# Attention and gated MLP on one core: the planner's due time for loads of q and k, from the fifth pair on

## The chip, the cores and the metric

The kernel runs on one core of one Trainium2 chip. The metric is the time of one execution on the device in microseconds (us). The core's engines are PE (TensorE; the loading of its weights is shown apart as PEld), ACT (ScalarE), DVE (VectorE), POOL (GpSimd) and SP (SyncE, which here only issues transfers). Each engine works through its own list of instructions in order; an instruction that waits for another engine or for a transfer holds all those behind it.

## The reference

For 8 batches with 8 heads, 576 positions and head size 64, the heads' outputs go side by side into a gated MLP:

```python
q_rot, k_rot = rotate(q), rotate(k)                  # x1*cos - x2*sin, x1*sin + x2*cos
scores = q_rot @ k_rot.transpose(0, 1, 3, 2) / np.sqrt(D)
attn = np.exp(scores - np.max(scores, axis=-1, keepdims=True))
attn = attn / (np.sum(attn, axis=-1, keepdims=True) + 1e-09)
x = (attn @ v).transpose(0, 2, 1, 3).reshape(B, S, H * D)
h = np.maximum(x @ w_in, 0.0)
u, v = h[..., :d_ff // 2], h[..., d_ff // 2:]
v_n = (v - mean(v)) / np.sqrt(var(v) + 1e-06)
v_s = np.einsum('ts,bsd->btd', w_spatial, v_n) + b_spatial[None, :, None]
out = (u * v_s) @ w_out
```

## The kernel before

**The work.** Heads are taken two at a time: four pairs in each batch, 32 in all, `pairs[i]`, numbered 0 to 31. For each pair `prepare(i)` makes q and k ready, `attention(i)` does the scores, the softmax and the values, and after every fourth pair `mlp(b)` does the MLP of the batch, whose steps run beside the attention of the next batch. Most numbers are split into a rounded high part and the remaining low part, and products are made of the parts.

**The preparation of one pair** (from pair 3 on). Two transfers bring q and k into two stage buffers, `st{i}_0` for q and `st{i}_1` for k, 128 x 1152 numbers of 4 bytes each: the input half and its rotated half (line 306 issues every transfer by SP; in the trace `st<-in_qk_dram`). There are two stage buffers, so a load waits until the pair before is done with its own. Then POOL multiplies both halves by the tables (`rope`, L401) and adds them (`rope_sum`, L405), ACT rounds the sum to its high part (`round_hi`, L309), and POOL or DVE takes the low part (`rest_lo`, L312). Ten transfers copy the parts into the stacked operands `qs`, `ks` and `qz`, and the low part of k goes into `lk`. Only then can the pair's scores begin.

**The attention of one pair.** It goes in three chunks. For each tile PE makes the scores `sc` (L536, L546), DVE the negative row maximum `nmx` (L557), ACT the exponential `e` (L559). For each chunk and each of five blocks PE transposes the exponentials into `tp` (L576), ACT writes the high part `eh` from it (L587), DVE the low part `el` (L312; for the last, short block both go into one buffer named eh), and PE multiplies them by the values into `pv` (L600).

**The MLP of one batch.** PE makes `pa`, from which the norm comes (`vv`, `vn`), then `pb` (L767), which ACT turns into `u` (L770), then `pc` (L785), gated by DVE and POOL into `g`, and last `pd` (L800), which ACT copies into the output buffer `ob` (L803) for the transfer to memory. Four such buffers `ob{b}_0` to `ob{b}_3` are filled in two halves each.

**Buffers on PE's side.** The transposes `tp` and the MLP's `pa`, `pb`, `pc` and `pd` share three buffers, `pm`. One is free again when the last reader is done: ACT and DVE for `tp`, ACT for `pb` and `pd`. There are two buffers `sc` and one `pv`.

**What sets the order.** A planner writes the order of all instructions before the kernel runs. Every step is an `Op` with a cost for each engine that may do it and a `key`, its due time. `Program.run` plays the kernel through: whenever an engine is free, it takes the step with the smallest key among those whose inputs are ready and whose buffers can be had. A step's results count as ready after its cost and the engine's latency:

```python
LATENCY = {PE: 200, ACT: 142, DVE: 118, POOL: 95, DMA: 1700}
heapq.heappush(events, (now + chosen.costs[e] + LATENCY[e], n + 1, "done", chosen))
```

The times of this play only set the order; on the chip each instruction waits for its real inputs. The load of q or k has the cost 1640 and the key 20 * i - 27; for the norm, rope, sums and low parts the planner may also choose between POOL and DVE.

Of the kernel before, what the change touches and what calls it, by code (L numbers as in the profile page):

```python
# [17 lines left out]
S = 576  # L18
# [11 lines left out]
PE, ACT, DVE, POOL, DMA = "pe", "act", "dve", "pool", "dma"  # L30
LATENCY = {PE: 200, ACT: 142, DVE: 118, POOL: 95, DMA: 1700}
TO_PE = 105
SLOTS = {
    "stage": 2, "lk": 1, "vraw": 2, "vs": 2, "e2": 4, "e1": 2, "eh": 7, "rb": 1, "x32": 1, "xg": 7, "m": 4,
    "small": 3, "nmx": 3, "rt": 2, "sc": 2, "pv": 1, "pm": 3,
# [31 lines left out]
K_LOAD, K_ROPE, K_SUM, K_HIQ, K_LOQ, K_LOK, K_STACK, K_STACK2, K_V, K_VLO = 27, 8, 8, 9, 9, 11, 30, 8, -2, -9  # L67
# [20 lines left out]
class Buf:  # L88


    def __init__(self, pools, shape, dt, name):
        self.pools, self.shape, self.dt, self.name = pools.split(), shape, dt, name
        self.users, self.pool, self.slot, self.tile = 0, None, None, None
# [5 lines left out]
class Op:  # L99
    def __init__(self, costs, key, f, new, port):  # L100
        self.costs, self.key, self.f, self.new, self.port = costs, key, f, new, port
        self.eng = None
        self.waits, self.after, self.bufs = 0, [], []


class Program:
# [5 lines left out]
    def op(self, eng, ns, key, f, r=(), w=(), new=(), port=False):  # L112
        return self.either({eng: ns}, key, lambda e: f(), r, w, new, port)
# [23 lines left out]
    def run(self, make):  # L137
        free = {p: list(range(n)) for p, n in SLOTS.items()}
        ready = {e: [] for e in LATENCY}

        own = dict.fromkeys(SLOTS, 0)
        for o in self.ops:
            for b in o.new:
                own[b.pools[0]] += 1

        def place(bufs):

            taken = []
            for b in bufs:
                pool = next((p for n, p in enumerate(b.pools) if free[p] and not (n and own[p])), None)  # L150
                if pool is None:
                    for t in taken:
                        free[t.pool].insert(0, t.slot)
                    return False
                b.pool, b.slot = pool, free[pool].pop(0)
                taken.append(b)
            for b in bufs:
                own[b.pools[0]] -= 1
            return True

        busy = dict.fromkeys(LATENCY, False)
        held = dict.fromkeys(LATENCY, False)
        events = [(0, n, "ready", o) for n, o in enumerate(self.ops) if not o.waits]
        n, left = len(self.ops), len(self.ops)
        heapq.heapify(events)
        index = {o: k for k, o in enumerate(self.ops)}
        while events:
            now = events[0][0]
            while events and events[0][0] == now:
                _, _, what, o = heapq.heappop(events)  # L170
                if what == "ready":
                    for n_e, e in enumerate(o.costs):
                        heapq.heappush(ready[e], (o.key + STEAL * n_e, index[o], o))
                elif what == "free":
                    busy[o] = held[o] = False
                elif what == "place":
                    free[o.pool].append(o.slot)
                else:
                    for b in o.bufs:
                        b.users -= 1  # L180
                        if not b.users:
                            late = TO_PE if b.pool in PSUM and o.eng != PE else 0
                            heapq.heappush(events, (now + late, n, "place", b))
                            n += 1
                    for a in o.after:
                        a.waits -= 1
                        if not a.waits:
                            late = TO_PE if PE in a.costs and o.eng != PE else 0
                            heapq.heappush(events, (now + late, n, "ready", a))
                            n += 1  # L190
            for e in LATENCY:
                if busy[e]:
                    continue
                passed, chosen = [], None
                while ready[e] and not chosen:
                    item = heapq.heappop(ready[e])
                    if item[2].eng:
                        continue
                    other = {DVE: POOL, POOL: DVE}.get(e)
                    if item[2].port and other and held[other]:  # L200
                        passed.append(item)
                    elif place(item[2].new):
                        chosen = item[2]
                    else:
                        passed.append(item)
                for item in passed:
                    heapq.heappush(ready[e], item)
                if chosen:
                    for b in chosen.new:
                        b.tile = make(b)  # L210
                    chosen.eng = e
                    chosen.f(e)
                    left -= 1
                    busy[e], held[e] = True, chosen.port
                    heapq.heappush(events, (now + chosen.costs[e], n, "free", e))
                    heapq.heappush(events, (now + chosen.costs[e] + LATENCY[e], n + 1, "done", chosen))
                    n += 2
        assert not left, "instructions wait for each other"
        return now
# [3 lines left out]
def tile_attention_gated_mlp(  # L223
# [33 lines left out]
    op = prog.op  # L257
# [47 lines left out]
    def load(dst, src):  # L305
        nc.sync.dma_start(out=dst, in_=src)  # L306
# [74 lines left out]
    def prepare(i):  # L381
        b, hp = pairs[i]
        key = 20 * i
        if i < WHOLE:
            return prepare_whole(i, b, hp, key)
        st = [Buf("stage", [P, 2 * S + TW], F32, f"st{i}_{j}") for j in range(2)]
# [19 lines left out]
            pair_op(S, key - K_SUM, f, first=eng, r=[(st[j], 1)], w=[(st[j], 0)])  # L406

        for j in range(2):
            op(DMA, 1640, key - K_LOAD, lambda j=j: load(st[j][:, :2 * S], qk[b, hp, j].rearrange("p c n -> p (c n)")), w=[(st[j], 0), (st[j], 1)], new=[st[j]])
        op(DMA, 910, key - K_LOAD + 1, lambda: load(vr.tile, v[b, hp]), w=[vr], new=[vr])  # L410
        for j, eng, part in ROPE0 if b == 0 else ROPE:
            if part is None:
# [435 lines left out]
    prepped, xs, chain = [], [], []  # L848
    op(POOL, 800, -26, setup, w=["ident", "bias", ("sums", 0, 0), ("sums", 1, 0), ("qz", 0), ("qz", 1), ("qs", 0, 0), ("qs", 1, 0)])
    prepare(0)  # L850
    for c in range(4):
        decode(DEC_V[c], win, (1, c), w_in[c * P:(c + 1) * P, 2 * HF:4 * HF])
# [7 lines left out]
    for i in range(len(pairs)):  # L860
        if i:
            prepare(i)
        (attention_plain if i < PLAIN else attention)(i)
        if i % NP == NP - 1:
            mlp(i // NP)
# [68 lines left out]
```

## Time and profile before

| | |
|---|---|
| median of 3 runs | 981.48 us (977.74 to 984.55) |
| profiled execution | 979.22 us |
| its span | 977.4 us |
| mean granted clock of TensorE | 0.999 of full speed |
| PE busy | 942.1 us, 96% |
| PEld busy | 853.3 us, 87% |
| ACT busy | 733.9 us, 75% |
| DVE busy | 672.1 us, 69% |
| POOL busy | 571.6 us, 58% |

The profile is of one execution, and its span leaves out what lies around it, here some 2 us. A busy share over the whole span mixes the start, when weights are decoded and PE waits, with the batches behind it, which look much alike, some 116 us each; a stretch of one batch says more. The lists of waits say for which instruction of which other engine an engine stood idle, how long in total, how often, and the longest.

### The profile page before, as it was taken

The page shows a single profiled execution, that of the slowest core. Times are in us where ns is not written, and L with a number is a line of the kernel's source. Part 1 is how long each engine was busy: PE and PEld are TensorE (multiplying, and loading weights), DVE is VectorE, ACT ScalarE, POOL GpSimd, SP SyncE. Part 2 cuts the span into 40 slices and gives each one's busy share as a digit, 9 for nine tenths or more (in the row PEclk, how much of TensorE's full clock was granted, in tenths as well). Part 3 has the DMA queues.
Part 4 walks back from the last instruction along what each step waited for, and adds up shares of the span by engine and source line. Part 5 has one row for each costly group of instructions (what it writes and reads, how often), then busy time and mean ns, then how long its engine had stood idle before and what let it go on. Part 6 is the DMA issues. An engine that isn't in the chain of part 4 may idle for free.

```text
span 977.4 us, 19421 instructions
## 1 busy us (share of the span) xinstructions
PE 942.1 (96%) x6618; PEld 853.3 (87%) x6618; DVE 672.1 (69%) x1486; ACT 733.9 (75%) x1827; POOL 571.6 (58%) x500
## 2 busy tenths in 40 slices
PE   4999999999999999999999999999999999999998
PEld 2455689998899989999899988999889998999998
DVE  6999898765866677675776658676686756767331
ACT  3778788777987779776897768877798677976452
POOL 5852445556757657774756766666576765672121
PEclk9999999999999999999999999999999999999999
DMA  7761733454344553345444444445524455330101
GB/s 295 221 197 52 209 100 108 130 128 140 99 139 117 153 150 101 111 120 165 120 130 108 118 151 126 118 128 149 139 76 132 126 156 145 98 93 17 62 2 49
DMA packets 54581, 121.56 MB, mean 124 GB/s; under 512 B 12881, under 2 KB 12881, under 8 KB 54482
## 3 DMA queue, kind: packets, MB, share of 16 engines
q1 hardware_dynamic: 54482, 120.32, 43.1%
q8 instruction: 53, 0.87, 0.4%
q14 instruction: 46, 0.38, 0.1%
HBM read 66.03 MB, written 9.58 MB: 77 GB/s over the span
## 4 chain that ended last, share of the span: by engine, by line
PE 59%; ACT 14%; DMA 9%; DVE 8%; POOL 4%; issue 3%; SPq 2%; DVEq 0%; ACTq 0%; POOLq 0%
PE pc L785 12%; PE sc L536 9%; PE pv L600 8%; PE tp L576 8%; PE pd L800 7%; PE pa L744 4%; PE pb L767 4%; ACT e L559 4%; DMA qs<-st 3%; POOL st L401 2%; ACT eh L587 2%; DVE nmx L557 2%; SPq L306 2%; PE sc L546 2%; ACT vv L827 2%
## 5 line engine op out<-in xcount | busy, mean ns | idle before, releaser
L587 ACT ACTIVATE eh<-tp 128x384 fp32r<-128x384 f32 (+1 forms) x504 | 217.5, 433 | 85.6 <-PE tp L576 69.5
L312 DVE TENSOR_TENSOR el<-tp,eh 128x384 fp32r<-128x384 f32 x336 | 185.9, 554 | 105.1 <-ACT eh L587 92.6
L559 ACT ACTIVATE e<-sc,nmx 128x576 f32<-128x576 f32 x288 | 213.0, 741 | 39.1 <-DVE nmx L557 36.7
L557 DVE TENSOR_REDUCE nmx<-sc 128x1 f32<-128x576 f32 x288 | 215.2, 749 | 31.8 <-PE sc L536 23.4
L576 PE MATMUL tp<-ident,e 128*128 128x128 f32 (+1 forms) x1176 | 197.1, 273 | 11.6 <-ACT ob L803 7.7
L576 PEld LDWEIGHTS tp<-ident,e 128*128 128x128 f32 (+1 forms) x1176 | 144.5, 138 | 30.4 <-ACT ob L803 9.1
L401 POOL TENSOR_TENSOR st<-st,tabq 128x576 f32<-128x576 f32 x55 | 77.7, 1427 | 135.9 <-DMA st<-in_qk_dram 131.0
L600 PE MATMUL pv<-eh,vs 128*128 128x384 f32 (+1 forms) x560 | 154.0, 316 | 0.1
L785 PE MATMUL pc<-wsp,vn 128*128 128x288 f32 x768 | 143.3, 304 | 0.8 <-DVE u L843 0.5
L767 PE MATMUL pb<-x,wi 128*128 128x288 f32 x768 | 142.3, 306 | 0.7 <-ACT u L770 0.7
L800 PE MATMUL pd<-g,wo 128*128 128x288 f32 x768 | 140.8, 304 | 0.0
L744 PE MATMUL pa<-wi,x 128*128 128x512 f32 x448 | 133.0, 407 | 0.0
L536 PE MATMUL sc<-ks,qs 128*128 128x288 f32 x580 | 123.2, 302 | 0.0
L785 PEld LDWEIGHTS pc<-wsp,vn 128*128 128x128 f32 x768 | 115.0, 189 | 3.4 <-DVE u L843 0.9
L710 POOL TENSOR_TENSOR x<-x,rb 128x576 f32<-128x576 f32 x31 | 44.3, 1429 | 123.7 <-DVE x L615 93.4
L767 PEld LDWEIGHTS pb<-x,wi 128*128 128x128 f32 x768 | 112.3, 189 | 4.4 <-PE pb L767 1.4
L800 PEld LDWEIGHTS pd<-g,wo 128*128 128x128 f32 x768 | 113.5, 189 | 2.6
L600 PE MATMUL pv<-el,vs 128*64 128x384 f32 (+1 forms) x448 | 113.7, 295 | 0.0
L536 PE MATMUL sc<-lk,qz 128*128 128x288 f32 x522 | 111.9, 295 | 0.0
L600 PEld LDWEIGHTS pv<-eh,vs 128*128 128x128 f32 x560 | 97.7, 188 | 5.8 <-DVE x L615 1.6
L312 DVE TENSOR_TENSOR eh<-tp,eh 64x256 fp32r<-64x256 f32 (+1 forms) x168 | 59.8, 356 | 61.4 <-ACT eh L587 52.3
L536 PEld LDWEIGHTS sc<-ks,qs 128*128 128x128 f32 x580 | 93.1, 189 | 6.3 <-ACT e L559 0.8
(180 smaller groups left out, 1559.2 us busy)
## 6 DMA issues: line engine op xcount, KB each, us to landing
st<-in_qk_dram SPq DMA_DIRECT2D x63, 576.0 KB
ks<-st SPq DMA_DIRECT2D x116, 160.0 KB
qs<-st SPq DMA_DIRECT2D x116, 144.0 KB
vr<-in_v_dram SPq DMA_DIRECT2D x32, 320.0 KB
out_dram<-ob SPq DMA_DIRECT2D x32, 288.0 KB
qz<-st SPq DMA_DIRECT2D x58, 144.0 KB
ws<-in_w_spT_dram SPq DMA_DIRECT2D x2, 576.0 KB
st<-in_qk_dram SPq DMA_DIRECT2D x2, 288.0 KB
```

The lines of the kernel that those rows point to most:

```text
L312: eng.tensor_tensor(out=lo, in0=src, in1=hi.bitcast(F32), op=ALU.subtract)
L401: f = lambda e: e.tensor_tensor(out=st[j][:, cols], in0=st[j][:, cols], in1=(tabs if j else tabq)[:, cols], op=ALU.mult)
L536: nc.tensor.matmul(pt[:, c * 512:c * 512 + HALF], lhsT=lhsT, rhs=rhs[:, k0 + c * HALF:k0 + (c + 1) * HALF], start=(n == 0), stop=(n == len ...
L557: op(DVE, 665, key + K_MAX, lambda: nc.vector.tensor_reduce(out=nmx.tile, in_=tops(), op=ALU.max, axis=AX.XY, negate=True), r=[pt], w=[nmx ...
L559: op(ACT, 730, key + K_EXP, lambda: nc.scalar.activation(e[:, e0:e0 + S].rearrange("p (c n) -> p c n", c=2), tops(), AF.Exp, bias=nmx.tile ...
L576: nc.tensor.transpose(out=tp[:e.shape[1], m * P:m * P + P], in_=e, identity=ident)
L587: nc.scalar.activation(h, p, AF.Copy)
L600: nc.tensor.matmul(pv[0:rows, c1:c2], lhsT=vs[:, kt, h, vp, :], rhs=part[:, c1:c2], start=(kt == 0 and n == 0 and c1 == 0), stop=last)
L744: nc.tensor.matmul(pm.tile, lhsT=lhsT, rhs=win[1, d][:, j, :], start=(d == 0 and n == 0), stop=(d == 3 and n == len(todo) - 1))
L767: nc.tensor.matmul(pm[:, :HALF], lhsT=win[0, d][:, i, f * P:(f + 1) * P], rhs=x[d][:, at:at + HALF], start=(d == 0 and n == 0), stop=(d == ...
L785: nc.tensor.matmul(pm[:, :HALF], lhsT=lhsT, rhs=rhs, start=(t == 0 and n == 0), stop=(t == 4 and n == 1))
L800: nc.tensor.matmul(pm[:, :HALF], lhsT=wout[d,][:, i, m * P:(m + 1) * P], rhs=gs[d][:, at:at + HALF], start=(d == 0 and n == 0), stop=(d == ...
```

## The change

The planner's `Op` gets a number `late`, zero by default, and a step's results count as ready so much later. The loads of q and k get 1500 ns from the fifth pair (i = 4) on: for the planner their data are there 1640 + 1700 + 1500 = 4840 ns after the issue instead of 3340. No instruction of the chip is added or taken away.

```diff
@@ -30,6 +30,7 @@
 PE, ACT, DVE, POOL, DMA = "pe", "act", "dve", "pool", "dma"
 LATENCY = {PE: 200, ACT: 142, DVE: 118, POOL: 95, DMA: 1700}
 TO_PE = 105
+LATE = 1500
 SLOTS = {
     "stage": 2, "lk": 1, "vraw": 2, "vs": 2, "e2": 4, "e1": 2, "eh": 7, "rb": 1, "x32": 1, "xg": 7, "m": 4,
     "small": 3, "nmx": 3, "rt": 2, "sc": 2, "pv": 1, "pm": 3,
@@ -99,7 +100,7 @@
 class Op:
     def __init__(self, costs, key, f, new, port):
         self.costs, self.key, self.f, self.new, self.port = costs, key, f, new, port
-        self.eng = None
+        self.eng, self.late = None, 0
         self.waits, self.after, self.bufs = 0, [], []
 
 
@@ -213,7 +214,7 @@
                     left -= 1
                     busy[e], held[e] = True, chosen.port
                     heapq.heappush(events, (now + chosen.costs[e], n, "free", e))
-                    heapq.heappush(events, (now + chosen.costs[e] + LATENCY[e], n + 1, "done", chosen))
+                    heapq.heappush(events, (now + chosen.costs[e] + LATENCY[e] + chosen.late, n + 1, "done", chosen))
                     n += 2
         assert not left, "instructions wait for each other"
         return now
@@ -406,7 +407,8 @@
             pair_op(S, key - K_SUM, f, first=eng, r=[(st[j], 1)], w=[(st[j], 0)])
 
         for j in range(2):
-            op(DMA, 1640, key - K_LOAD, lambda j=j: load(st[j][:, :2 * S], qk[b, hp, j].rearrange("p c n -> p (c n)")), w=[(st[j], 0), (st[j], 1)], new=[st[j]])
+            o = op(DMA, 1640, key - K_LOAD, lambda j=j: load(st[j][:, :2 * S], qk[b, hp, j].rearrange("p c n -> p (c n)")), w=[(st[j], 0), (st[j], 1)], new=[st[j]])
+            o.late = LATE if i >= 4 else 0
         op(DMA, 910, key - K_LOAD + 1, lambda: load(vr.tile, v[b, hp]), w=[vr], new=[vr])
         for j, eng, part in ROPE0 if b == 0 else ROPE:
             if part is None:
```

In the changed file the lines behind the new constant are one further down, and those from the loads on two.

The instructions are the same, but for three operations of pairs 3 to 7 and batch 0 that go from DVE to POOL. The lists have 3454 rows on PE, and about 200 of them stand elsewhere; 509 on SP, one of them elsewhere. The order differs from about 107 us of the trace before on. From the third batch on the differences repeat in every batch, one kind for each of its four pairs, and the end from about 870 us on is as it was.

In the rows below a name is followed by its batch, pair, head, chunk, block or half, and a serial number at the end. Before, on ACT, in batch 4's output (`pd4`, `ob4`) beside pairs 23 and 24, while pair 25 is prepared:

```order
L617 ACTIVATE avt23_1_9744<-pv23_1_9627 64x384
L803 ACTIVATE ob4_2_9752<-pd4_20_9702 128x288
L587 ACTIVATE eh23_2_3_9779<-tp23_2_3_9770 128x384
L559 ACTIVATE e2_24_1_9784,sums0_68<-sc24_0_3_9754,nmx24_0_3_9774 128x576
L309 ACTIVATE st25_0_9645<-st25_0_9645 128x576
L803 ACTIVATE ob4_2_9752<-pd4_21_9746 128x288
L587 ACTIVATE eh23_2_4_9808<-tp23_2_4_9800 64x2x128
L587 ACTIVATE eh23_2_4_9808<-tp23_2_4_9800 64x128
L587 ACTIVATE eh24_0_0_9817<-tp24_0_0_9811 128x384
L803 ACTIVATE ob4_3_9844<-pd4_30_9795 128x288
L309 ACTIVATE st25_1_9671<-st25_1_9671 128x576
```

The rounding of pair 25's q stands ahead of the copy of `pd4_21`. The same place on ACT in the changed kernel:

```order
L589 ACTIVATE eh23_2_3_9778<-tp23_2_3_9749 128x384
L561 ACTIVATE e2_24_1_9789,sums0_68<-sc24_0_3_9768,nmx24_0_3_9776 128x576
L805 ACTIVATE ob4_2_9737<-pd4_21_9743 128x288
L310 ACTIVATE st25_0_9638<-st25_0_9638 128x576
L589 ACTIVATE eh23_2_4_9811<-tp23_2_4_9799 64x2x128
L589 ACTIVATE eh23_2_4_9811<-tp23_2_4_9799 64x128
L589 ACTIVATE eh24_0_0_9820<-tp24_0_0_9807 128x384
L805 ACTIVATE ob4_3_9844<-pd4_30_9793 128x288
L589 ACTIVATE eh24_0_1_9851<-tp24_0_1_9840 128x384
L561 ACTIVATE e2_24_1_9789,sums0_68<-sc24_0_4_9824,nmx24_0_4_9838 128x576
L310 ACTIVATE st25_1_9660<-st25_1_9660 128x576
```

The copy now stands ahead of the rounding of q, and two more rows stand ahead of that of k. It is so at the pairs 9, 13, 17, 21, 25 and 29. Before, on ACT, two pairs earlier, while batch 4's `u` is made:

```order
L587 ACTIVATE eh21_2_3_8925<-tp21_2_3_8916 128x384
L559 ACTIVATE e2_22_1_8930,sums0_68<-sc22_0_3_8899,nmx22_0_3_8920 128x576
L309 ACTIVATE st23_0_8787<-st23_0_8787 128x576
L770 ACTIVATE u4_3_8945<-pb4_30_8891 128x288
L587 ACTIVATE eh21_2_4_8954<-tp21_2_4_8947 64x2x128
L587 ACTIVATE eh21_2_4_8954<-tp21_2_4_8947 64x128
L587 ACTIVATE eh22_0_0_8963<-tp22_0_0_8957 128x384
```

The rounding of pair 23's q stands ahead of `u4_3`. The same place on ACT in the changed kernel:

```order
L589 ACTIVATE eh21_2_3_8924<-tp21_2_3_8915 128x384
L561 ACTIVATE e2_22_1_8929,sums0_68<-sc22_0_3_8898,nmx22_0_3_8919 128x576
L772 ACTIVATE u4_3_8939<-pb4_30_8890 128x288
L589 ACTIVATE eh21_2_4_8952<-tp21_2_4_8945 64x2x128
L589 ACTIVATE eh21_2_4_8952<-tp21_2_4_8945 64x128
L310 ACTIVATE st23_0_8787<-st23_0_8787 128x576
L589 ACTIVATE eh22_0_0_8967<-tp22_0_0_8955 128x384
```

It now stands behind `u4_3` and the two pieces of `eh21_2_4`, and so at the pairs 11, 15, 19, 23, 27 and 31. Before, on POOL, in the preparation of pair 22:

```order
L401 TENSOR_TENSOR st22_0_8311<-st22_0_8311,tabq_65 128x576 x2
L312 TENSOR_TENSOR vn_73<-vv4_0_8264,vn_73 128x512
L405 TENSOR_TENSOR st22_0_8311<-st22_0_8311 128x576
L401 TENSOR_TENSOR st22_1_8337<-st22_1_8337,tabs_64 128x576 x2
L312 TENSOR_TENSOR vn_73<-vv4_1_8297,vn_73 128x512
L405 TENSOR_TENSOR st22_1_8337<-st22_1_8337 128x576
L312 TENSOR_TENSOR st22_0_8311<-st22_0_8311 128x576
```

The last two rows are the sum of k and the low part of q. The same place on POOL in the changed kernel:

```order
L402 TENSOR_TENSOR st22_0_8311<-st22_0_8311,tabq_65 128x576
L313 TENSOR_TENSOR vn_73<-vv4_0_8264,vn_73 128x512
L402 TENSOR_TENSOR st22_0_8311<-st22_0_8311,tabq_65 128x576
L402 TENSOR_TENSOR st22_1_8337<-st22_1_8337,tabs_64 128x576
L406 TENSOR_TENSOR st22_0_8311<-st22_0_8311 128x576
L313 TENSOR_TENSOR vn_73<-vv4_1_8297,vn_73 128x512
L402 TENSOR_TENSOR st22_1_8337<-st22_1_8337,tabs_64 128x576
L313 TENSOR_TENSOR st22_0_8311<-st22_0_8311 128x576
L406 TENSOR_TENSOR st22_1_8337<-st22_1_8337 128x576
```

The low parts of the norm (`vn`) stand between the ropes, and the sum of k stands behind the low part of q; so it is at the pairs 10, 14, 18, 22, 26 and 30.

## Rows read from the trace of the kernel before

**Rows 1.** The page's first part: busy us, share of the span, instructions of each engine.

```profile
PE 942.1 (96%) x6618; PEld 853.3 (87%) x6618; DVE 672.1 (69%) x1486; ACT 733.9 (75%) x1827; POOL 571.6 (58%) x500
```

**Rows 2.** Windows: busy us (instructions) of each engine, PE clock, DMA share, GB/s.

```profile
core 0: us, PE busy (x) PEld busy (x) DVE busy (x) ACT busy (x) POOL busy (x), PEclk, DMA share, GB/s
...
100.00:227.00 127.00, 123.65 (x881) 110.69 (x877) 99.05 (x208) 97.63 (x242) 68.31 (x57) 1.00 0.49 135
573.00:689.00 116.00, 113.70 (x826) 107.47 (x826) 79.43 (x182) 91.59 (x231) 75.69 (x65) 1.00 0.46 127
```

**Rows 3.** Waits of PE from 100 to 900 us: total us, times, longest.

```profile
PE tp L576 <- ACT ob L803: 7.7, 6, 1.5
PE tp L576 <- ACT u L770: 2.1, 3, 0.8
PE tp L576 <- DVE eh L312: 0.6, 1, 0.6
PE pc L785 <- DVE u L843: 0.5, 1, 0.5
PE pb L767 <- ACT u L770: 0.5, 1, 0.5
```

**Rows 4.** Waits of POOL and of ACT over the whole span.

```profile
POOL st L401 <- DMA st<-in_qk_dram: 131.0, 24, 7.9
ACT st L309 <- POOL st L405: 15.0, 24, 1.6
```

**Rows 5.** Timeline: start us, us, engine, line, operation [idle before <- releaser], 686.6 to 692 us.

```profile
686.75 0.65 PE L800 MATMUL pd<-g,wo 128*128 128x288 f32 x3
...
687.77 0.68 ACT L309 ACTIVATE st<-st 128x576 fp32r<-128x576 f32 x1 [1.60 <-POOL st L405]
688.36 0.39 ACT L803 ACTIVATE ob<-pd 128x288 f32<-128x288 f32 x1
688.65 1.23 ACT L587 ACTIVATE eh<-tp 64x256 fp32r<-64x256 f32 x3
...
688.80 0.55 PE L576 MATMUL tp<-ident,e 128*128 128x128 f32 x3 [1.40 <-ACT ob L803]
...
689.33 0.72 DVE L312 TENSOR_TENSOR eh<-tp,eh 64x256 fp32r<-64x256 f32 x2 [3.29 <-ACT eh L587]
...
691.13 0.49 PE L576 MATMUL tp<-ident,e 128*128 128x128 f32 x3
...
691.38 0.65 PE L800 MATMUL pd<-g,wo 128*128 128x288 f32 x3
...
691.87 0.33 PE L600 MATMUL pv<-eh,vs 128*128 128x384 f32 x1
```

**Rows 6.** Timeline, 630.2 to 631.7 us.

```profile
630.28 0.68 ACT L309 ACTIVATE st<-st 128x576 fp32r<-128x576 f32 x1 [0.91 <-POOL st L405]
630.87 0.39 ACT L770 ACTIVATE u<-pb 128x288 f32<-128x288 f32 x1
631.16 0.65 ACT L587 ACTIVATE eh<-tp 64x256 fp32r<-64x256 f32 x2
...
631.31 0.55 PE L576 MATMUL tp<-ident,e 128*128 128x128 f32 x3 [0.73 <-ACT u L770]
```

**Rows 7.** Timeline of SP: loads of pairs 22 and 25, first copies of pair 25's k.

```profile
589.88 1.78 SPq L306 DMA_DIRECT2D st<-in_qk_dram  x2
...
677.23 2.55 SPq L306 DMA_DIRECT2D st<-in_qk_dram  x2
...
692.75 1.10 SPq L306 DMA_DIRECT2D ks<-st  x2
```

**Rows 8.** Timeline of POOL: ropes of pairs 22 and 25, low part of pair 22's q.

```profile
593.64 2.83 POOL L401 TENSOR_TENSOR st<-st,tabq 128x576 f32<-128x576 f32 x2 [5.84 <-DMA st<-in_qk_dram]
...
604.46 1.44 POOL L312 TENSOR_TENSOR st<-st 128x576 fp32r<-128x576 f32 x1
...
682.16 2.82 POOL L401 TENSOR_TENSOR st<-st,tabq 128x576 f32<-128x576 f32 x2 [7.83 <-DMA st<-in_qk_dram]
```

**Rows 9.** Timeline of ACT: both pieces of pair 22's k rounded.

```profile
607.09 0.82 ACT L309 ACTIVATE st<-st 128x576 fp32r<-128x576 f32 x2
```

**Rows 10.** Timeline of PE: first score of pair 25.

```profile
705.45 0.43 PE L536 MATMUL sc<-ks,qs 128*128 128x288 f32 x2
```

## What the change will do: a prediction

> **What bounds the kernel now.** I read the busy shares first. PE works 942.1 of 977.4 us [rows 1], and in a settled stretch of one batch 113.70 of 116 us, while ACT has 91.59 and DVE 79.43 [rows 2]. So PE sets the time, and since the change keeps every instruction, it can pay only by taking idle time from PE; idle time of POOL, ACT or DVE counts only where PE is behind it.
>
> Next I read what PE waits for between 100 and 900 us [rows 3]. Two lines carry it: the transposes (L576) wait six times for ACT's output copy ob (L803), 7.7 us in all, and three times for ACT's u (L770), 2.1 us. The smaller lines below them all lie in batch 0, before 227 us. Asked apart, the stretch from 227 us on has the first two lines and no other. The rest of PE's 35 idle microseconds lies at the start and at the end, where the order of the instructions that run then is hardly touched.
>
> Why does PE wait for an output copy? The stall at 688.80 us shows it [rows 5]. PE begins its last three pd matmuls before it at 686.75 and then has no work until 688.80, when the transposes of pair 24, chunk 0 start, released by the ob copy that began at 688.36. The copy frees one of three pm buffers. The copy itself had its input long before. It stood behind the rounding of pair 25's q (L309, 687.77), which had waited 1.60 us for POOL's sum (L405). ACT takes its queue in order. POOL in turn was late because the load of that pair was late: POOL's ropes (L401) wait for q and k loads 24 times, 131.0 us in all, and ACT's roundings for POOL's sum 24 times, 15.0 us [rows 4]. At 631.31 us the same thing happens with u in the place of ob: 0.91 us of waiting on ACT, 0.73 on PE [rows 6].
>
> How late is the load? The one for pair 25 is issued at 677.23 [rows 7], and POOL's first rope on it starts at 682.16, ending a wait of 7.83 us for just that [rows 8]: 4.93 us. For pair 22 it is 589.88 to 593.64, 3.76 us. The plan counts 1640 + 1700 ns = 3.34 us. By it the rounding stood ready before the copy, so the copy was put behind it; on the chip it is not ready, by 1.6 us there.
>
> **The change part by part.** The plan now counts 4.84 us for those loads, close to the 4.93 at the place that stalls.
>
> *Six places with ob (pairs 9, 13, ... 29).* In the new order ACT's ob copy stands ahead of the rounding that waits. The pm buffer is then free as soon as pd is done, and the transposes no longer wait: six waits, 7.7 us [rows 3].
>
> *Three places with u (the pairs 4n+3).* The order puts u and the two pieces of eh ahead of the rounding: 2.1 us [rows 3].
>
> *What the restart costs besides.* From the start of the three pd matmuls at 691.38 to the next matmul's at 691.87 is 0.49 us; from 686.75 the next could have started at 687.24, and it started at 688.80. That is 1.56 us where the row's idle time says 1.40 [rows 5]: 0.16 us more per stall, by nine stalls 1.4 us. Together 7.7 + 2.1 + 1.4 = 11.2 us.
>
> *What is late next.* ACT still waits at the ob places, now with the copy done. Behind its rounding stand the two short pieces of eh, and behind them DVE's subtraction (689.33, 0.72 us), which frees the pm buffer for the transposes now at 691.13 [rows 5]. Without the copy in front, eh starts at 688.36 instead of 688.65, and DVE is done at 689.33 - 0.29 + 0.72 = 689.76. With PE earlier by 1.56, those transposes want the buffer at 691.13 - 1.56 = 689.57. So 0.2 us comes back, if POOL is as late as it is now. The bounds are nothing (POOL a little earlier) and 0.3 us (one more handover), by six places 0 to 1.8; I take 0.8. At the u places eh stands ahead of the rounding as well, so nothing comes back there.
>
> *The rounding that is now later.* Pair 25's q is rounded later by the copy, 0.39 us [rows 5], and at the u places by u and eh, 0.39 + 0.65 us [rows 6]. Who waits for that? The copies of q and k into the stacked operands, and then the pair's first score on PE. For pair 25 the first k copies are issued at 692.75 [rows 7] and the score starts at 705.45 [rows 10]: some 12 us of cover. I cost it at nothing; without the cover it would be at most 1.04 us at each of 12 places.
>
> *POOL and DVE, pairs 4n+2.* Sum of k moves behind the low part of q on POOL. Before, the low part ends at 604.46 + 1.44 = 605.90 [rows 8] and ACT comes to its roundings at 607.09 [rows 9] without waiting. If POOL does the same work in the new order and ends its last piece then, 1.2 us of slack remains. Nothing, as long as the load lands as it does.
>
> *SP.* Its order keeps all 509 entries, one of them moved; no queue of transfers is held by the change. Whether a q or k load is issued earlier depends on when its stage buffer is free, which is not new.
>
> *Batch 0 (105 to 185 us).* Here the reordering is wide, and three operations go from DVE to POOL. PE is idle for 127.00 - 123.65 = 3.35 us between 100 and 227 us [rows 2], so a gain is at most about 3. A loss of the same size is as near, from a new wait as long as the longest two there are [rows 3]. I take 0, with both ends kept.
>
> **Sum.** The profiled execution took 979.22 us, against the runs' median of 981.48, 2.26 lower and within their spread. 979.22 - 11.2 + 0.8 = 968.8 on its own footing; with the 2.26 put back, 971.0 us, a ratio of 0.989. Batch 0 (3 either way) and the part that comes back (0.8 down, 1.0 up) give 967 to 975.
>
> One rule of the Trainium skill speaks against the change. Its page "DMA: Bandwidth & Descriptors", section "Anatomy of one DMA — SWDGE (gpsimd) path", fits one transfer as 2.0 us plus its bytes over 436,000 per us. For 589,824 bytes I estimate 3.35 us from it, which is the old plan's figure to 10 ns; by it the old order would be right and the sum nothing. That section is about another issuing path, and the trace differs: 4.93 and 3.76 us [rows 7, 8].
>
> **The rivals.** *The wait moves on.* The rounding still blocks ACT at the six ob places, and if what is behind it (eh, DVE, the pm buffer) is 0.5 to 1.2 us late instead of 0.2, then 3 to 7 of the 11.2 us are lost again. For it: three pm buffers turn fast, and ACT's idle 1.60 us has not gone anywhere [rows 5]. Against it: the 0.2 us worked out above. Time: 975 to 980.
>
> *The plan counts too much.* Half of the loads land in about 3.8 us like pair 22's [rows 7, 8]; for them 4.84 is wrong by 1.1. If that delays work that PE needs at as many places as it frees, the sum is nothing: 978 to 984. Against it: PE has no wait on the loads' chain other than through ACT's queue [rows 3], and the cover of 12 us.
>
> *Slower: sum of k at the pairs 4n+2 (7 places from pair 6 on).* It now stands last on POOL, with 1.2 us of slack before ACT reaches the rounding of k. A load that lands in 4.96 us instead of 3.76 uses it up; pair 25's took 4.93. Beyond it, each microsecond holds ACT, whose queue there has the softmax's work for PE behind it. To eat the 10.4 us of net gain takes 1.5 us at each of seven places, so loads of 6.5 us; at 7.1 us it is 7 x 2.1 = 15 us, 984 on the profile's footing and 986 for the median. The rows hold no such load.
>
> **How the numbers follow.** The forecast, 967 to 975, has 0.62: mechanism and rows agree nine times. The wait that moves on has 0.23, the plan that counts too much 0.07, slower 0.08. About 1% is what a measurement of this kernel can tell from no change, so faster starts below 971.7: two thirds of the forecast's case, 0.41. Slower by over 1% is the last rival, 0.08 with little of the others; the rest, 0.51, lies within. The range 966 to 979.5 holds the forecast and nearly all of the wait that moves on, and leaves out the slower case and most of the plan that counts too much.
>
> **What would show it.** In the profile after, PE's line of transposes waiting for ob should be gone or under 1 us, that for u gone, and ACT's waits of L309 for L405 still there, some 10 us or more, with ob and u ahead of them. PE busy in a batch should be near 115 of 116 us. A new line, transposes waiting for DVE's eh, of up to 2 us would be the part that comes back; over 3 us it is the first rival. Waits of ACT on the rounding of k at the pairs 4n+2, with PE behind, would be the last one. I am wrong if PE's total wait is as before, or if the loads themselves land later now.

## The result, and the profile after

The changed kernel took 968.24 us in the median (967.76 to 968.79) against 983.01 of the kernel before beside it: a ratio of 0.9851, interval 0.9816 to 0.9885. Its profiled execution took 968.03 us, before 979.22. So it is faster by 1.1 to 1.8%; 971.0 was forecast, within 966.0 to 979.5. One execution of one experiment below (after, transfer added: 1008.68 us at a granted clock of 0.884) was in a slower state of the chip and is left out of the ratios.

The page's first part, answering to [rows 1]: PE does the same work in a span 11.1 us shorter.

```profile
PE 940.3 (97%) x6618; PEld 853.8 (88%) x6618; DVE 667.7 (69%) x1484; ACT 734.7 (76%) x1828; POOL 572.3 (59%) x501
```

Windows of the kernel after, columns as in [rows 2]: batch 0 has 1.51 us without PE instead of 3.35, a settled stretch 0.17.

```profile
100.00:226.00 126.00, 124.49 (x892) 112.17 (x893) 95.86 (x210) 99.66 (x251) 69.86 (x59) 1.00 0.51 139
455.00:569.00 114.00, 113.83 (x829) 107.97 (x828) 79.88 (x183) 92.09 (x232) 76.04 (x65) 1.00 0.48 130
```

Waits of PE after, from 100 to 890 us. The two lines that led [rows 3] are gone. One of the two waits of the first line, 0.65 us, is told of below; the other lies in batch 0.

```profile
PE tp L578 <- DVE eh L313: 0.8, 2, 0.7
PE tp_2a L637 <- DVE et_1b L646: 0.7, 1, 0.7
PE pc L787 <- DVE u L845: 0.3, 1, 0.3
...
```

Waits of POOL and ACT after, over the whole span, against [rows 4]. POOL waits for late loads as ever (some of its waits now bear the name of another transfer), but ACT's waits for POOL's sum are down to 10 from 24: it comes to the rounding later, with other work done first. Only one of the ten, 1.32 us at pair 25, is at a place with ob or u ahead of q's rounding. Five, of 1.23 to 1.25 us, are at the pairs 12, 16, 20, 24 and 28, where before had 0.2 to 0.6: POOL comes to their first rope 5.5 to 5.8 us after the issue of the load instead of 3.9 to 4.0. No wait of PE follows those five.

```profile
POOL st L402 <- DMA st<-in_qk_dram: 109.8, 18, 7.3
...
POOL st L402 <- DMA rt23d<-rt: 8.8, 1, 8.8
...
ACT st L310 <- POOL st L406: 8.6, 10, 1.3
```

The place with `u`, against [rows 6], first on ACT (timeline of the kernel after): u, both pieces of eh, then the rounding of pair 23's q, without a wait. PE's transposes of pair 22 start at 623.01, with no idle time ahead of them.

```profile
621.85 0.41 ACT L772 ACTIVATE u<-pb 128x288 f32<-128x288 f32 x1
622.80 0.66 ACT L589 ACTIVATE eh<-tp 64x256 fp32r<-64x256 f32 x2 [0.55 <-PE tp L578]
623.49 0.69 ACT L310 ACTIVATE st<-st 128x576 fp32r<-128x576 f32 x1
```

A place with `ob` as five of the six look now, pair 21's (timeline of ACT after): the copy, and right behind it the rounding, which by then has its input.

```profile
564.69 0.40 ACT L805 ACTIVATE ob<-pd 128x288 f32<-128x288 f32 x1
564.98 0.68 ACT L310 ACTIVATE st<-st 128x576 fp32r<-128x576 f32 x1
565.55 1.17 ACT L589 ACTIVATE eh<-tp 64x256 fp32r<-64x256 f32 x3
```

The sixth, pair 25's, against [rows 5] (timeline of all engines after). The copy is done early and PE starts pair 24's transposes at 678.94 with no wait. The rounding still waits 1.32 us, and behind it stand eh, DVE's subtraction, and PE's next transposes, 0.65 us late.

```profile
678.15 0.41 ACT L805 ACTIVATE ob<-pd 128x288 f32<-128x288 f32 x1
...
678.94 0.49 PE L578 MATMUL tp<-ident,e 128*128 128x128 f32 x3
...
679.88 0.69 ACT L310 ACTIVATE st<-st 128x576 fp32r<-128x576 f32 x1 [1.32 <-POOL st L406]
...
680.48 1.16 ACT L589 ACTIVATE eh<-tp 64x256 fp32r<-64x256 f32 x3
...
681.15 0.73 DVE L313 TENSOR_TENSOR eh<-tp,eh 64x256 fp32r<-64x256 f32 x2 [3.30 <-ACT eh L589]
...
682.03 0.52 PE L578 MATMUL tp<-ident,e 128*128 128x128 f32 x3 [0.65 <-DVE eh L313]
```

Pair 25 differs from pair 21 mostly by when its load is issued (timeline of SP after): 9.67 us ahead of the copy, behind a transfer for qz that held SP for 2.02 us. At the pairs 13, 21 and 29 it is issued 11.0 to 11.1 us ahead of the copy.

```profile
665.01 2.02 SPq L307 DMA_DIRECT2D qz<-st  x1
...
668.49 1.59 SPq L307 DMA_DIRECT2D st<-in_qk_dram  x2
```

**Where the time came from.** The same instruction can be found in both traces, so the span is cut at two of them: the first transposes of pair 4 and the first score of pair 8. The second stretch is batch 0, the third all that follows, up to the start of the last matmul.

| us | to pair 4 | batch 0 | the rest |
|---|---|---|---|
| before | 109.03 | 104.17 | 760.41 |
| after | 110.34 | 102.30 | 749.80 |
| difference | +1.31 | -1.87 | -10.61 |

### The profile page after: what moved, and what is told of

Its sections match the earlier page's. It is cut to its first block, busy times and chain, and to the rows that moved or that the text cites. A ratio compares the mean times of both kernels' runs of the same rounds, so it can differ in the third digit from the quotient of the medians.

```text
span 966.3 us, 19411 instructions
## 1 busy us (share of the span) xinstructions
PE 940.3 (97%) x6618; PEld 853.8 (88%) x6618; DVE 667.7 (69%) x1484; ACT 734.7 (76%) x1828; POOL 572.3 (59%) x501
## 4 chain that ended last, share of the span: by engine, by line
PE 77%; ACT 9%; DVE 8%; DMA 3%; issue 2%; POOL 0%; SPq 0%; ACTq 0%; DVEq 0%
PE sc L538 12%; PE pc L787 12%; PE pv L602 11%; PE tp L578 11%; PE pd L802 10%; PE pb L769 9%; PE pa L746 5%; ACT e L561 3%; PE sc L548 3%; DVE nmx L559 2%; PE pv L675 2%; ACT eh L589 2%; ACT vv L829 2%; DVE el L313 1%; PE tp L637 1%
```

## The experiments

Each, but for one repeat, changes a line or two of the changed kernel or of the one before. The table has each profiled execution, cut as above, and the ratio on record of the run's times to those of the kernel before beside it, which is not that of the two medians alone.

| run | to pair 4 | batch 0 | the rest | ratio (interval) |
|---|---|---|---|---|
| pairs 4n+1 | 111.40 | 106.67 | 751.48 | 0.9916 (0.9887 to 0.9945) |
| pairs 4n+3 | 110.36 | 105.47 | 756.13 | 0.9965 (0.9942 to 0.9989) |
| even pairs | 110.27 | 104.64 | 762.28 | 1.0001 (0.9983 to 1.0019) |
| pairs 4 to 8 | 111.00 | 102.28 | 759.44 | 0.9966 (0.9945 to 0.9987) |
| before, half loads | 110.42 | 103.81 | 748.28 | 0.9875 (0.9849 to 0.9902) |
| after, half loads | 109.77 | 102.07 | 749.19 | 0.9868 (0.9842 to 0.9893) |
| before, transfer added | 110.50 | 106.21 | 791.81 | 1.0401 (1.0383 to 1.0418) |
| after, transfer added | 110.30 | 103.93 | 759.98 | 1.0007 (0.9993 to 1.0021) |
| after, again | 110.81 | 102.26 | 749.68 | 0.9889 (0.9861 to 0.9916) |
| 4 to 8 and odd pairs | 110.94 | 102.47 | 748.79 | 0.9877 (0.9838 to 0.9917) |
| 700 ns | 109.72 | 106.12 | 748.99 | 0.9915 (0.9895 to 0.9935) |
| 3000 ns | 116.14 | 104.15 | 758.05 | 1.0031 (1.0017 to 1.0046) |

**The theory** is that of the prediction: a late load holds a rounding on ACT, and PE loses what stands behind it there. **The rival** is that the wider reordering (PE's rows, POOL, batch 0) makes the gain. The first four runs are the change in parts, which together are the whole.

```diff
-            o.late = LATE if i >= 4 else 0
+            o.late = LATE if i >= 9 and i % 4 == 1 else 0
```

> Loads count 1500 ns longer for the pairs 9, 13, ... 29 alone. In the order only 19 rows of ACT move (the copy ob ahead of the rounding of q, and what follows it); PE, DVE, POOL and SP keep the order of before. If the gain is ACT's queue, PE's six waits for ob (7.7 us in the profile of before) go, with their restart lag 1.0 us, and at most 1 us comes back as a wait for DVE's eh: the span is some 8 us shorter than before's 977.4, about 969.5. If the gain is made by the wider reordering of PE and POOL, which this kernel does not have, the span stays within 2 us of 977.4.

The rest took 8.93 us less than before, although by the traces all 6618 instructions of PE stand in the order of before, and 19 of ACT do not. The waits of PE from 215 to 900 us hold one line, without ob:

```profile
PE tp L578 <- ACT u L772: 2.1, 2, 1.3
```

The span was 973.4 all the same, not 969.5: the stretches to pair 4 and of batch 0, whose order is that of before, took 4.87 us longer than in before's profile. The median of the run's six executions is 972.49 us, 10.4 under that of before beside it.

```diff
+            o.late = LATE if i >= 9 and i % 4 == 3 else 0
```

> Loads count 1500 ns longer for the pairs 11, 15, ... 31 alone. 18 rows of ACT move (u and eh ahead of the rounding of q), one of POOL, two of SP. If the gain is ACT's queue, PE's three waits for u (2.1 us) go, with 0.5 us of restart lag, nothing comes back: 2.6 us off the span, 974.8. The six waits for ob stay, 7 to 9 us. The other theory: no change.

The rest took 4.28 us less. The waits of PE in the same stretch hold ob alone; u is gone:

```profile
PE tp L578 <- ACT ob L805: 6.9, 6, 1.7
```

0.8 of the 4.28 is that the ob waits came out smaller in this execution; what was expected, 2.6, is the most of it. Here too PE keeps the order of before.

```diff
+            o.late = LATE if i >= 9 and i % 2 == 0 else 0
```

> Loads count 1500 ns longer for the pairs 10, 12, 14, ... 30 alone. 250 rows of PE, 66 of ACT, 29 of POOL move, but ob and u stay behind the rounding of q at all twelve places. If the gain is ACT's queue, nothing is gained: the span is within 1.5 us of 977.4, and the six waits for ob and three for u are there, 9 to 11 us together. If the wider reordering makes the gain, most of the 11 us is here: about 968.

Nothing was gained; the rest took 1.87 us more. But the six ob waits did not stay as expected. Waits of PE, same stretch:

```profile
PE tp L578 <- DVE el L313: 8.0, 5, 2.5
PE tp L578 <- ACT u L772: 2.6, 3, 1.2
PE tp L578 <- ACT ob L805: 0.9, 1, 0.9
```

The first line is the same fault under another name, as the timeline of this kernel shows at pair 25: the rounding now stands ahead of one more eh, and PE waits for what DVE makes of that.

```profile
689.87 0.68 ACT L310 ACTIVATE st<-st 128x576 fp32r<-128x576 f32 x1 [2.45 <-POOL st L406]
690.46 0.47 ACT L589 ACTIVATE eh<-tp 128x384 fp32r<-128x384 f32 x1
...
690.97 0.56 DVE L313 TENSOR_TENSOR el<-tp,eh 128x384 fp32r<-128x384 f32 x1 [2.80 <-ACT eh L589]
...
691.58 0.44 PE L578 MATMUL tp<-ident,e 128*128 128x128 f32 x2 [1.98 <-DVE el L313]
```

The name in a wait's row is the last in a chain; the head of the chain is found by following the releasers back.

```diff
+            o.late = LATE if 4 <= i < 9 else 0
```

> Loads count 1500 ns longer for the pairs 4 to 8 alone. Only the stretch from 105 to 213 us is in another order (160 rows of PE, 48 of ACT; three operations go from DVE to POOL). From the trace after the change, PE gains 1.9 us between the first transposes of pair 4 and the first score of pair 8, counted against the same stretch before. I expect 2 us off the span, 975.5, the ob and u waits behind 213 us as before; the theory of the wider reordering in all batches gives the same here, the ACT theory alone would give less than 1 us, since the longest waits of batch 0 are not for ob.

Batch 0 took 102.28 us, as in the whole change, against 104.17 to 106.67 in the four executions of the old order there (before and the three runs above). So the theory misses a part: here the reordering itself gains. It is more than the three operations from DVE to POOL of the section on the change: by the traces five instructions go from DVE to POOL, four from POOL to DVE and one from DVE to ACT, and PE's rows move. Which of these gains was not tested apart. The waits of PE from 109 to 213 us in this run are four short ones; the kernel before had 1.8 us there, 1.6 of it in [rows 3].

```profile
PE pc L787 <- DVE u L845: 0.3, 1, 0.3
PE sc L538 <- ACT e L561: 0.2, 1, 0.2
PE tp L578 <- DVE eh L313: 0.2, 1, 0.2
PE pv L602 <- ACT x L681: 0.2, 1, 0.2
```

Next the root itself, the load, in both orders. Half of each load:

```diff
-load(st[j][:, :2 * S], qk[b, hp, j].rearrange("p c n -> p (c n)"))
+load(st[j][:, :2 * S] if i < 5 else st[j][:, :S],
+     qk[b, hp, j].rearrange("p c n -> p (c n)") if i < 5 else qk[b, hp, j, :, 0])
 ...
-in0=st[j][:, cols]
+in0=(st[j] if i < 5 or not part.start else tabs if j else tabq)[:, cols]
```

> The order of before, with its ob and u behind the rounding, but from the sixth pair on the loads of q and k bring only the first half of each row (288 KB instead of 576), and the second rope takes its input from the table, so scores from then on are wrong; every engine does as much work as before. If the late load is the root, a load that lands about 1 us earlier cuts each of PE's nine waits by as much: 9.8 us before, about 2.5 left, the span some 8 us shorter, near 969 to 970. If the place of ob and u on ACT cost time for another reason (the order itself, buffers), the waits stay and the span is within 2 us of 977.4.

> The changed order with the same half loads (the same part of the computation left out). If the late load is the root, little is left to gain: the 0.8 us of waits for DVE's eh, so 965 to 966 for the span (after: 966.3). The gap between the two orders, 11 us with whole loads, should be 3 to 4 us here. The other theory keeps the gap at 8 us or more.

In the order of before, PE has no wait at all left from 215 to 900 us, and the rest took 748.28 us; the changed order took 749.19. With prompt loads the old order is as good as the new one: the gap between the two, 10.6 us in the rest with whole loads, is gone, where 3 to 4 us were expected to be left. From the issue of q's load to POOL's first rope the mean at the pairs 4n+1 was 5.47 us in before and is 3.90 here; ACT's waits for the sum fell from 15.0 us [rows 4] to

```profile
ACT st L309 <- POOL st L405: 1.3, 6, 0.4
```

At the pairs 4n+2 the same means are 3.84 and 3.11 us, 0.73 apart. With whole loads the load takes 1.6 us longer at the pairs 4n+1 than at 4n+2, for the same bytes. More is under way there: while pair 25's load was (first window below, kernel before), the core moved 300 GB/s for 4.93 us, some 1,480 KB; while pair 22's was, 235 GB/s for 3.76 us, some 880 KB.

```profile
677.23:682.16 4.93, 4.93 (x44) 4.93 (x43) 2.96 (x7) 3.45 (x10) 0.00 (x0) 1.00 0.98 300
589.88:593.64 3.76, 3.76 (x30) 3.45 (x29) 3.26 (x13) 2.87 (x9) 0.00 (x1) 1.00 0.87 235
```

By the fit on the page "DMA: Bandwidth & Descriptors" of the Trainium skill, section "Anatomy of one DMA — SWDGE (gpsimd) path", which is for transfers that GpSimd issues, I estimate 0.68 us for the 294,912 bytes left out. The 0.73 at the pairs 4n+2, where SP issues, agrees. Its 2.0 us for what does not depend on bytes is less than the 2.4 to 2.5 that the same estimate leaves there of 3.11 and 3.84.

The other way, a transfer added ahead of each q load from pair 5 on:

```diff
+pad = dr.tile([P, S], F32, tag="pad", name="pad", bufs=1)
 ...
-lambda j=j: load(st[j][:, :2 * S], ...)
+lambda j=j: (j or i < 5 or load(pad, qk[0, 0, 0, :, 0]), load(st[j][:, :2 * S], ...))
```

> The order of before, with a transfer of 288 KB from memory to memory put ahead of each q load from the sixth pair on. It holds the load back; I take 1 us. If the late load is the root, each of the nine waits grows by that, 9 us, and places with little slack (the pairs 4n+3 that did not stall) join: the span 986 to 992. The other theory: under 2 us more.

> The changed order with the same added transfer. At the six ob places the rounding still holds eh and with it DVE and the buffer; the slack there is 0 to 0.4 us, so up to 0.6 to 1 us at each comes back as PE's wait for DVE's eh or el, 4 to 6 us: the span 970 to 973. At the u places eh stands ahead of the rounding and nothing should come back. If the change made PE independent of the load altogether, the span stays at 966 to 967.

The load came 0.8 to 1.1 us later (means of 6.30 us at 4n+1 and 5.77 at 4n+3, before 5.47 and 4.64). The old order lost 31.4 us in the rest, far more than the 9 to 15 expected, the new one 10.2. Waits of PE in the old order, 215 to 930 us:

```profile
PE tp L578 <- ACT ob L805: 16.3, 6, 3.1
PE tp L578 <- ACT u L772: 10.4, 5, 2.8
```

Together they are 16.9 us more than the 9.8 of before, and PE's idle time in the rest grew by 17.3. At the six ob places a wait grew by 1.4 us on average for a load that came 0.8 later; why it grew by more was not tested. The other 14.1 of the 31.4 us are longer busy time of PE: its clock fell, as the last section tells.

Waits of PE in the new order, 215 to 900 us:

```profile
PE pc L789 <- DVE el L315: 2.6, 2, 1.6
PE tp L580 <- DVE eh L315: 2.0, 4, 0.9
PE tp L580 <- DVE sm L828: 0.5, 1, 0.5
PE pd L804 <- DVE el L315: 0.5, 1, 0.5
```

5.6 us of waits, as expected, but the stretch is 10.2 longer: PE's idle time in the rest grew by 5.2 and its busy time by 5.0, at a granted clock of 1.00. Those 5.0 are not broken down. The change makes PE less dependent on the load, not independent.

The last four are on the figure and the choice of pairs.

> The changed kernel once more, beside the kernel before on another chip. If the ob and u copies no longer depend on when the loads land, its executions should lie within 2 us of each other, where those of before spread over 5 us or more, since each late load there reaches PE. If the spread has another source, both spread alike.

The span was 966.6. Three executions lay between 968.14 and 970.14 us, the fourth at 973.24, a spread of 5.1 against 4.1 of before. So this doesn't show that the change takes away the spread. What the record shows beside it is the clock: the fourth had a mean granted clock of 0.993, the others 0.999 to 1.0, and the two runs with half loads and the next one have one such execution each, 971.99 to 973.15 us at 0.992 or 0.993. Only profiled executions left a trace, so where the clock fell in these is open. The ratio here, 0.9889, is the forecast's 0.989.

```diff
+            o.late = LATE if 4 <= i < 9 or i % 2 else 0
```

> Loads count 1500 ns longer for the pairs 4 to 8 and, from 9 on, for the odd pairs alone: the three parts that gained by themselves, without the even pairs. By the sum of the parts it is as fast as the changed kernel, span 965 to 968. If the even pairs' part is needed beside the others (PE's order fitted to ACT's), it is slower by 2 us or more.

The span was 966.0, and the median, 967.28, is 2 us under that of the changed kernel beside it, which their spreads don't tell apart. The even pairs' part adds nothing.

```diff
-LATE = 1500
+LATE = 700
```

> 700 ns instead of 1500, from the fifth pair on: 4.04 us counted for loads that take 3.8 to 5.5. In its order ob and u stand ahead of the rounding at eleven of the twelve places; the twelfth, pair 31, did not stall before. If only the order at those places counts, the span is 965 to 969 as with 1500. If the due time itself must match the landing, 4.04 us is too short for the pairs 4n+1 and a good part of the gain is missing: 970 to 974.

In the rest 700 ns does as well as 1500 (748.99 us). The pairs 4n+1 were counted at 4.04 us and took 4.76 in this run, so the due time need not match; the copies have to stand ahead. But batch 0, where PE's instructions stand in the order of before, took 106.12 us, as in the old order. The gain is smaller by that.

```diff
-LATE = 1500
+LATE = 3000
```

> 3000 ns instead of 1500: 6.34 us counted, more than any load took. Ob and u stand ahead at all twelve places, but some 800 rows of PE are in another order. If only those places count, the span is 965 to 969. If a due time past the landing costs (the rounding and all behind it pushed back, PE's scores later), it is above 972.

Slower than before. The start took 4.7 to 7.1 us longer than in the other runs, most of it by a lower clock (last section). In the rest ob waits are back at another place, behind the rounding of k, five of them from 335 to 800 us:

```profile
PE tp L578 <- ACT ob L805: 3.2, 5, 0.7
```

That is less than half of the 8.3 us by which the rest is longer than after the change; what the other rows moved cost was not taken apart.

## Why the prediction was right, point by point

*What bounds it.* Right: PE's idle time in the rest, added up, fell from 11.2 to 1.9 us, and the stretch from 760.41 to 749.80. The other 1.4 us came off PE's busy time, as much as was forecast for the restart.

*The six ob places, three u places and the restart.* 11.2 us less 0.8 were forecast for these, 10.4; the rest gave 10.61, and by parts 8.93 and 4.28, with the even pairs' 1.87 against them, 11.3. The restart cost shows by itself too: at the u place of [rows 6], 0.73 us of idle time, PE's lead over before grew by 0.89, from 7.42 to 8.30.

*What is late next.* The size of 0.8 came out, the way it comes did not. 0.2 was expected at each of six places. The wait, 0.65 us, is at pair 25 alone; PE, 9.86 us ahead at that place, is 8.84 ahead after it, so it cost 1.0. The load there was issued 1.4 us later, against the copy, than at the pairs 13, 21 and 29, and took 668.49 to 674.25, 5.76 us, where theirs took 5.4. The repeat of the changed kernel has the same one wait, 0.8 us. At the other five the rounding found its input ready behind the copy. So the sign that ACT's waits would stay, some 10 us with ob and u ahead of them, failed: 8.6 us are left, 1.32 of them at such a place.

*The rounding that is now later, POOL at the pairs 4n+2, SP.* Nothing was lost there: no wait of ACT on these pairs' roundings, and no wait of PE for a score's operands. The slower rival had no load long enough: the longest at these pairs took 4.3 us after the change. On SP a load did come to be issued later, at pair 25 as told.

*Batch 0.* This term was mis-sized. It was taken at 0 with 3 either way and is -1.87 against before's profile and -2.9 against the mean of the four executions of the old order. The waits there, 1.8 us, became four short ones. That the reordering gained is shown; by which of its moves is open.

*From the profile to the median.* 2.26 us were added to the sum as a fixed distance. They were not one: before's profile is of an execution that had come to pair 8's first score at 213.20 us, where three others with the same order there had 214.9 to 218.1. The changed kernel's median lies 0.2 us from its profile. 968.8 was the sum on the profile's footing, and 968.03 was measured. That it is so near is in part luck: batch 0 gave 1.87 us that were not counted, and the start, nearly all of it in the order of before, happened to take 1.31 longer. The 971.0 was 2.8 high: 2.05 by the distance, 0.6 by batch 0 and the start together, 0.2 by the rest.

*The rivals.* The wait that moves on came to 0.65 us of idle time and cost 1.0. The plan that counts too much had nothing to it at 1500, as the run without the even pairs shows, but at 3000 it is real.

## What to carry to other kernels

Where an engine works in order and a list of instructions is planned, a time that the plan has too short costs by what stands behind the waiting instruction, not by the wait itself: 131 us of waiting for loads on POOL cost PE 11. Look for the late transfer at the head of the chain and let work that frees buffers stand ahead of what waits for it; how far the plan's figure is raised matters less than what it lets pass, and too far is a loss. Before adding the distance between one profile and the median to a forecast, ask whether the change takes away what makes it.

## What the runs showed of the hardware that was not expected

The clock fell after most of the long stalls. In the old order with the added transfer PE stalls for 2 to 3 us, and in the 5 us around one such stall (290 to 295 us, PE busy for 2.91) the granted clock was 0.71. Windows of that run, the rest nearly whole and this stretch:

```profile
215.00:930.00 715.00, 686.77 (x4880) 647.49 (x4880) 470.69 (x1082) 539.66 (x1360) 436.62 (x372) 0.98 0.46 129
290.00:295.00 5.00, 2.91 (x12) 2.82 (x13) 1.27 (x3) 2.01 (x5) 5.00 (x4) 0.71 0.11 40
```

The mean of the execution was 0.987. I estimate from it and the span of 1012.3 us that some 13 us of PE's work were lost, which is nearly all of the 14.1 by which PE's busy time in the rest grew. So the added transfer cost the old order by its waits and almost as much again by the clock. A long stall does not always lower it: from 215 to 240 us, around a wait of 2.8 us, it stayed at 1.00; so it did in the kernel before, where the stalls from 100 us on were up to 1.5 us, and where the first score of all came after a wait of 10.0 us. What decides is not shown. With 3000 ns it fell to 0.51, about the lower of its two levels (1.2 GHz), after a stretch in which PE was busy for 7.79 of 10 us; the changed kernel has 9.89 and then 8.84 there, at full clock. Ten us at 0.51 lose 4.9 us of work, an estimate, which is most of the 4.7 to 7.1 by which that run's start was longer. Windows of the kernel with 3000 ns:

```profile
70.00:80.00 10.00, 7.79 (x48) 3.94 (x47) 9.39 (x16) 7.61 (x19) 1.69 (x2) 1.00 0.12 33
80.00:90.00 10.00, 8.44 (x29) 4.60 (x30) 5.88 (x11) 3.40 (x10) 1.57 (x3) 0.51 0.12 31
```
